# Resident slices of the second expert weights, and engines of some small steps, in an attention and mixture-of-experts kernel

## The chip, the cores and the metric

The kernel runs on one core of a Trainium2 chip. Five engines share the work: TensorE (PE in the rows, with its weight loads as PEld), VectorE (DVE), ScalarE (ACT), GpSimd (POOL) and SyncE (SP), which here only issues DMAs. The metric is device time in microseconds (us), the median of several runs.

## The reference

Three stages follow each other. `x` is 8 batches × 8 heads × 512 tokens × 64, `state` is 8 × 8 × 32 × 64.

```python
scores = scale * x @ state.T;  a = softmax(scores, -1);   xread = a @ state
scores2 = scale * state @ x.T; a2 = softmax(scores2, -1); sread = a2 @ x
y = concat([xread, sread], axis=2)          # 8 batches x 544 rows x 512
h = y @ w_in                                # 512 -> 2048
g = where(h >= 1, h, where(h <= -1, 0, (h + 1) ** 2 / 4))
z = g @ w_out                               # 2048 -> 512, 4352 rows
logits = z @ phi                            # 32 slots: 8 experts x 4
d = softmax(logits, 0);  slot_input = d.T @ z
slot_out[e] = relu(slot_input[e] @ w1[e]) @ w2[e]     # w1: 512 x 1024, w2: 1024 x 512
out = softmax(logits, 1) @ slot_out
```

The softmax over all rows (`axis 0`) means that no row of the output can be made before all rows have passed `h`; the two expert layers then work on 32 slots only, and the output is a small matrix product for 4352 rows of 512.

## The kernel before

**Loop over batches.** `b` runs from 0 to 8. For `b` from 0 to 7 a step works on the 512 token rows of a batch; `b` = 8 (`b == B`, the "state block") works on the 256 state rows of all batches. Inside, `m` runs over 16 blocks of 128 hidden columns (`hstep`). For each `m`, TensorE sums `h` into one of three PSUM banks; ScalarE makes `c = relu(h / 2 + 1/2)`; `c` is squared; VectorE makes `g = min(max(h, 1), c)` (L592) and later transposes `g` (L612, `tstep`). Who squares is a letter for each `m` in the strings `gv0` (`b` = 0), `gv1`, `gv`, `gv7` (`b` = 7) and `gvS` (state block): `S` is ScalarE, `E` is GpSimd (L568), and `B` is a third form in which VectorE clamps `h` (L563), ScalarE squares and VectorE adds (L596).

**First two steps.** While `b` = 0 runs, the 64-bit words of `w_in` and `w_out` are turned into floats (`conv_win`, `conv_wo`: lines 154 to 172, and byte copies on ScalarE and GpSimd). Tables (`cpos`, `at0`, `V0`, `E0`, `T0`, `attA`, `Vn`, `x2` and others) say at which `m` a piece of this work is written down. For `b` = 0 and 1 and for everything from `b` = 8 on, a scheduler makes each engine's order from that; for `b` = 2 to 7 TensorE's order is as written.

**State block.** `wsplit(m)` splits 128 columns of `w_in` into a high part (a copy, L519 or on ScalarE) and a low part (a subtraction, L520), for three products each in `hstep` (L546). The two letters of `wS[m]` name the engines of the two parts: `A` ScalarE, `D` VectorE, `P` GpSimd. There are two buffers, so the split for `m` can begin when the products for `m` − 2 are done.

**Last stage.** Weights come in slices of 1 MB (128 × 2048 floats): 16 of `w1`, and 16 of `w2`, of which 0 to 7 make columns 0 to 255 of `slot_out` (half 0) and 8 to 15 the columns 256 to 511 (half 1). Six `w2` slices, the last six of `order`, are loaded in the large tile `gp` as soon as the transposed `g` there has been used (`ends`); the other 26 slices are streamed through places that `give` frees. All loads and nearly all stores go through SP's one queue, in program order. `slot_out(dh)` sums the eight slices of a half (tile `SO`, L1088), resident ones first, and spreads the sum to all partitions (`SR`, L1095). `combine` then makes output rows: four products of 128 rows into four banks (`oV`, `oH`, `oX`, `oE`), two copied out by VectorE (L1128) and two by ScalarE, and stores (L1132). `c0` and `c1` make half rows (256 columns, 1 KB of an output row) for pairs of batches; `cw` makes whole rows for the batches in `whole`, for which both halves must be there. The string `so` sets the order: `0` and `1` are a slice of half 0 and half 1, `c` is a pair of half rows of half 0; what is left follows in the order half 1, `c0`, `cw`, `c1`.

```python
r0 = CFG["r0"]
kept = [list(range(8 - r0, 8)), list(range(10 + r0, 16))]
order = [i for i in range(16) if i not in kept[0] + kept[1]] + kept[0] + kept[1]
```

With `r0` = 0 the resident slices are 10 to 15, all of half 1.

Of the kernel before, what the change touches and what calls it, by code (L numbers as in the profile page):

```python
# [13 lines left out]
PSUM = bass.MemoryType.PSUM  # L14


CFG = {'no': 1, 'nl': 0, 'n0': (1, 12), 'nw': 512, 'nj': 'CABD', 'cw': (2, 2, 2, 4, 5, 6, 6, 7, 8, 8, 9, 11, 12, 13, 14, 15), 'pr': (0, 4, 6), 'a0n': 5, 'w1p': (), 'r0': 0, 'sw': 1, 'whole': (4, 5, 6, 7), 'em': 8, 'lE': (0, 5, 8, 11), 'sV': (0, 4, 9, 12), 'sE': (7, 11, 15), 'sS': (1, 3, 5, 7), 'sN': 13, 'sM': (14, 14), 'gv7': 'EESESSSEESSSEEEE', 'cpos': (0, 0, 1, 2, 2, 3, 3, 7, 8, 10, 10, 10, 14, 14), 'at0': (4, 4, 7, 7, 9, 13, 14, 14, 14, 15), 'lP0': ((0, 1), (1, 0), (3, 0), (3, 1)), 'lP1': ((1, 0), (1, 1), (2, 0), (2, 1), (3, 0)), 'gv1': 'EEEEEEEEEESEEEES', 'f32': (0, 1, 2, 3), 'wsm': 14, 'xsP': 1, 'eng': ('PE',), 'wt8': (7, 8, 9, 10, 11, 12, 13, 14), 'wte': 'DA', 'wb': 12, 'gv6': (3, 5, 15), 'lP': ((0, 0), (0, 1), (1, 0), (2, 0), (3, 1)), 'attA': (3, 3, 9, 9, 9, 10, 10, 12), 'attB': (1, 11, 11, 12, 13), 'attN': (14, 15), 'dv': (3, 7, 8), 'fl': -0.484375, 'hp': 2000, 'att7': (3, 5, 6, 7, 8, 10), 'og': 1, 'n3': 1, 'n3m': 10, 'wS': ('DP', 'PP', 'AD', 'PD', 'AP', 'DP', 'AP', 'AD', 'AD', 'DP', 'AD', 'AP', 'AP', 'AD', 'PD', 'AD'), 'xsm': 12, 'k0': 0, 'rg': 6, 'spg': 0, 'att0': 6, 'att': 7, 'V0': (1, 2, 4), 'Vn': (1, 2, 10), 'Vx': 12, 'wn': 'H', 'wsev': 'adad', 'conv': (4, 8, 9, 11, 12, 13, 19, 21, 24, 26, 28, 32, 36, 40, 44, 48, 52, 56, 60), 'todo': [1, 1, 1, 2, 0, 0, 0, 3, 0, 0, 2, 2, 1, 1, 0, 0], 'E0': ((0, 7), (0, 14), (0, 15), (1, 1)), 'T0': ((0, 9), (0, 14), (1, 1), (1, 2)), 'sm0': 6, 'E': 1, 'sm': 1, 'tqB': (5, 9, 13), 'GP': 0, 'pe': (3,), 'psH': 3, 'gtpX': (0, 7), 'tq0': (13, 15), 'keep': (2, 3, 4, 5), 'x2': (1, 0), 'natm': 1, 'warm': 26, 'bounce7': (0, 3), 'split': 1, 'wt': 0, 'so': '1011110001000010c1cc1', 'smm': (0, 0, 1, 2, 8, 10, 12), 'tqv': (), 'tqvm': 0, 'first': 'x', 'apath': 2, 'f32c': 1, 'place': 1, 'attm': (3, 6, 7, 8, 9, 12), 'subPm': True, 'loDm': False, 'bounce': (0, 1, 2, 3), 'bq': ('s', 's'), 'xq': 's', 'nat': ((1, 11), (2, 2), (2, 3), (2, 11), (3, 2), (3, 4), (3, 9), (4, 2), (4, 3), (4, 9), (5, 2), (5, 3), (5, 9), (6, 2), (6, 4), (6, 9)), 'subP': (1,), 'mulD': (), 'loD': (), 'qlag': 0, 'gv0': 'SSEEEEEESEEEEEEE', 'gv': 'EEEEEEESEEEESEEE', 'gvS': 'BEBBBBBBBBBSBEBB'}


@with_exitstack  # L20
def kernel(
# [20 lines left out]
    def pool(name, bufs, **kw):  # L42
        return ctx.enter_context(tc.tile_pool(name=name, bufs=bufs, **kw))
# [6 lines left out]
    small = pool("small", 2)  # L50
    psH = pool("psH", CFG["psH"], space=PSUM)
    psE = pool("psE", 1, space=PSUM)
    psV = pool("psV", 1, space=PSUM)
    psX = pool("psX", 5 - CFG["psH"], space=PSUM)
    dram = pool("dram", 1, space=bass.MemoryType.DRAM)
# [58 lines left out]
    def group(calls, after=(), chain=False):  # L114

        first = mm(**calls[0])  # L116
        for i in after:
            tc.add_manual_dep(first.ins, i.ins.name, SYNC, reason="side by side")
        with tc.high_priority(CFG["hp"]):
            last = first  # L120
# [5 lines left out]
    def act(out, in_, func=ACTF.Copy, **kw):  # L126
        return nc.scalar.activation(out=out, in_=in_, func=func, **kw)  # L127
# [21 lines left out]
    def words(i, dst):  # L149

        w = stage[i].bitcast(U32).rearrange("p (f w) -> p f w", w=2)
        if i in CFG["dv"]:
            d = dst.bitcast(U32)
# [9 lines left out]
        r = rim.bitcast(U8).rearrange("p (f w) -> p f w", w=4)  # L163
        act(r[:, :, 0], b[:, :, 3], scale=2.0 ** -5, bias=CFG["fl"])
        if i in CFG["pr"]:
            nc.gpsimd.tensor_copy(out=r[:, :, 3], in_=b[:, :, 7])
# [1025 lines left out]
```

## Time and profile before

| | us |
|---|---|
| runs | 482.29, 480.94, 481.89 |
| median | 481.89 |
| profiled execution | 481.2 |
| its span, first to last instruction | 479.4 |

| engine | busy us | share of the span |
|---|---|---|
| PE | 435.4 | 91% |
| DVE | 374.4 | 78% |
| ACT | 289.2 | 60% |
| POOL | 239.5 | 50% |

The table is an average over stages that have different limits: DMA is full in the first 48 us and again from about 380 us on, VectorE is full from 36 to 72 us, and TensorE is full from 60 to 400 us. 93.00 MB go through SP's queue. What a change in a stage is worth has to be read in that stage. 1.8 us of the profiled execution lie outside its span.

### The profile page before, as it was taken

The page shows a single profiled execution, that of the slowest core. Times are in us where ns is not written, and L with a number is a line of the kernel's source. Part 1 is how long each engine was busy: PE and PEld are TensorE (multiplying, and loading weights), DVE is VectorE, ACT ScalarE, POOL GpSimd, SP SyncE. Part 2 cuts the span into 40 slices and gives each one's busy share as a digit, 9 for nine tenths or more (in the row PEclk, how much of TensorE's full clock was granted, in tenths as well). Part 3 has the DMA queues.
Part 4 walks back from the last instruction along what each step waited for, and adds up shares of the span by engine and source line. Part 5 has one row for each costly group of instructions (what it writes and reads, how often), then busy time and mean ns, then how long its engine had stood idle before and what let it go on. Part 6 is the DMA issues. An engine that isn't in the chain of part 4 may idle for free.

```text
span 479.4 us, 10721 instructions
## 1 busy us (share of the span) xinstructions
PE 435.4 (91%) x4336; PEld 247.3 (52%) x4336; DVE 374.4 (78%) x667; ACT 289.2 (60%) x528; POOL 239.5 (50%) x217
## 2 busy tenths in 40 slices
PE   5689899999999999999999999999999997999850
PEld 2433345456565565655556555565557685435330
DVE  2999999896999998999799899878878655430260
ACT  1876996647775875886697587565654464220350
POOL 4243447865774973885497388464146231220030
PEclk9899999999999999999999999999999999999995
DMA  8999822011403613342351346025053598999698
GB/s 304 420 420 420 338 89 89 19 71 27 151 18 132 250 44 133 114 196 61 127 210 46 133 144 252 3 90 176 2 211 124 198 404 335 349 424 414 255 355 314
DMA packets 19809, 94.21 MB, mean 197 GB/s; under 512 B 1840, under 2 KB 6320, under 8 KB 11184
## 3 DMA queue, kind: packets, MB, share of 16 engines
q1 hardware_dynamic: 19504, 93.00, 51.0%
q8 instruction: 34, 0.56, 0.5%
q0 software_dynamic: 256, 0.52, 0.5%
q14 instruction: 15, 0.12, 0.1%
HBM read 80.41 MB, written 13.11 MB: 195 GB/s over the span
## 4 chain that ended last, share of the span: by engine, by line
PE 49%; DVE 28%; DMA 6%; ACT 5%; issue 5%; POOL 4%; ACTq 0%; SPq 0%; POOLq 0%; DVEq 0%
PE h L538 17%; DVE gp L612 6%; DVE g L592 5%; PE h L546 5%; PE E L116 3%; DMA w<-in_w_dram 3%; PE FV L122 3%; PE V L116 3%; PE h L1053 3%; POOL c L568 2%; PE h L529 2%; PE FX L122 2%; DVE mx L294 2%; DMA wb<-in_won_dram 2%; DVE z L335 1%
## 5 line engine op out<-in xcount | busy, mean ns | idle before, releaser
L538 PE MATMUL h<-a,v 128*128 128x512 f32 x672 | 175.5, 405 | 2.3 <-DVE g L592 2.0
L568 POOL TENSOR_TENSOR c<-c 128x512 f32<-128x512 f32 x106 | 114.6, 1084 | 97.1 <-ACT c L127 95.3
L538 PEld LDWEIGHTS h<-a,v 128*128 128x128 f32 x672 | 120.3, 188 | 77.9 <-issue 19.5
L127 ACT ACTIVATE c<-h,half 128x512 f32<-128x512 f32 x128 | 88.3, 691 | 71.0 <-PE h L538 54.6
L592 DVE SCALAR_TENSOR_TENSOR g<-h,c 128x512 f32<-128x512 f32 x112 | 74.7, 668 | 20.1 <-POOL c L568 17.0
L612 DVE STREAM_TRANSPOSE gp<-g 128x512 f32<-128x512 f32 x112 | 78.0, 699 | 1.1
L485 POOL TENSOR_TENSOR v<-Vs,v 128x512 fp32r<-128x512 f32 x30 | 41.7, 1389 | 9.5 <-ACT Vs L127 9.5
L127 ACT ACTIVATE v<-V 128x512 fp32r<-128x512 f32 (+1 forms) x64 | 38.1, 602 | 8.1 <-PE V L122 4.1
L116 PE MATMUL V<-win,st_t 64*32 64x512 f32 x64 | 34.0, 611 | 4.1 <-ACT att L127 3.7
L122 PE MATMUL V<-win,st_t 64*32 64x512 f32 x448 | 36.3, 612 | 0.0
L122 PE MATMUL FX<-gp,dR 32*32 32x512 f32 x512 | 35.6, 598 | 0.0
L122 PE MATMUL FV<-gp,dR 32*32 32x512 f32 x496 | 35.4, 597 | 0.0
L529 PE MATMUL h<-spare,v 128*128 128x512 f32 x64 | 32.5, 644 | 2.2 <-DVE gp L592 2.0
L122 PE MATMUL E<-g,wp 128*32 128x512 f32 x168 | 29.5, 602 | 0.0
L116 PE MATMUL E<-g,wp 128*32 128x512 f32 x56 | 29.1, 602 | 0.0
L337 POOL TENSOR_TENSOR att<-att,z 128x512 f32<-128x512 f32 x16 | 17.2, 1076 | 18.1 <-DVE z L336 18.1
L546 PE MATMUL h<-XSh,v 128*128 128x256 f32 x128 | 25.2, 289 | 0.1
L127 ACT ACTIVATE spare<-wb 128x512 uint8<-128x512 uint8 x32 | 24.0, 785 | 1.0 <-DMA wb<-in_won_dram 1.0
L1128 DVE COPY o<-oV 128x512 f32<-128x512 f32 x5 | 3.5, 691 | 26.5 <-PE oH L122 26.3
L529 PEld LDWEIGHTS h<-spare,v 128*128 128x128 f32 x64 | 11.9, 202 | 20.2 <-issue 13.5
L546 PEld LDWEIGHTS h<-XSh,v 128*128 128x128 f32 x128 | 20.2, 189 | 2.6 <-DVE g L592 0.8
L375 POOL TENSOR_TENSOR a<-att,a 128x512 fp32r<-128x512 f32 x14 | 19.6, 1418 | 1.1 <-ACT a L127 1.1
(245 smaller groups left out, 813.9 us busy)
## 6 DMA issues: line engine op xcount, KB each, us to landing
w<-in_w_dram SPq DMA_DIRECT2D x22, 1024.0 KB, 9.6
xn<-in_xn_dram SPq DMA_DIRECT2D x8, 1024.0 KB, 4.8
wb<-in_won_dram SPq DMA_DIRECT2D x8, 1024.0 KB, 5.0
xs<-in_xs_dram SPq DMA_DIRECT2D x7, 1024.0 KB, 4.8
gp<-in_w_dram SPq DMA_DIRECT2D x6, 1024.0 KB, 7.4
gp<-in_wout_dram SPq DMA_DIRECT2D x5, 1024.0 KB, 11.7
wb<-in_win_dram SPq DMA_DIRECT2D x4, 1024.0 KB, 12.8
wo<-wb SPq DMA_DIRECT2D x8, 512.0 KB, 3.7
```

The lines of the kernel that those rows point to most:

```text
L116: first = mm(**calls[0])
L122: e = mm(**c)
L127: return nc.scalar.activation(out=out, in_=in_, func=func, **kw)
L337: (nc.vector if b in CFG["mulD"] else nc.gpsimd).tensor_tensor(out=t3, in0=t3, in1=z1.unsqueeze(2).to_broadcast([128, 16, 32]), op=ALU.mult)
L375: (nc.vector if b in CFG["loD"] or b > 1 and CFG["loDm"] else nc.gpsimd).tensor_tensor(out=lo[:, G, :], in0=raw[G], in1=hi[:, G, :], op=AL ...
L485: nc.gpsimd.tensor_tensor(out=lo[:, G, :], in0=Vs, in1=hi[:, G, :], op=ALU.subtract)
L529: mm(out=h, lhsT=Vt[0, c][0][:, G, 128 * mm_:128 * mm_ + 128], rhs=araw[0][G], start=(G == 0), stop=(G == 1))
L538: mm(out=h, lhsT=v[:, G, f], rhs=a[:, G, :], start=(k == 0), stop=(k == 5))
L546: mm(out=h, lhsT=w[:, j, :], rhs=x[:, j, :], start=(k == 0), stop=(k == 11))
L568: nc.gpsimd.tensor_tensor(out=c, in0=c, in1=c, op=ALU.mult)
L592: gI[b, m] = nc.vector.scalar_tensor_tensor(out=g, in0=h, scalar=1.0, in1=c, op0=ALU.max, op1=ALU.min)
L612: nc.vector.transpose(out=gd_of(b, m), in_=gT[b, m])
```

## The change

Only the table of settings is changed (one line of code; here its changed keys stand below each other).

```diff
 CFG = {
...
-'r0': 0, 'whole': (4, 5, 6, 7), 'so': '1011110001000010c1cc1',
+'r0': 3, 'whole': (6, 7),       'so': '111000000000ccc111111',
-'gv7': 'EESESSSEESSSEEEE', 'gvS': 'BEBBBBBBBBBSBEBB',
+'gv7': 'EESEESSEEESSEEEE', 'gvS': 'BEBBBEEESSSBEBBB',
-'gv0': 'SSEEEEEESEEEEEEE',
+'gv0': 'ESSESEEESEEEEEEE',
-'wS': ('DP', 'PP', 'AD', 'PD', 'AP', 'DP', 'AP', 'AD', 'AD', 'DP', 'AD', 'AP', 'AP', 'AD', 'PD', 'AD'),
+'wS': ('AP', 'PP', 'AD', 'AP', 'DP', 'DP', 'PP', 'DD', 'AP', 'DP', 'AD', 'AP', 'DD', 'AD', 'DD', 'DP'),
-'pr': (0, 4, 6), 'a0n': 5, 'x2': (1, 0), 'V0': (1, 2, 4), 'Vn': (1, 2, 10),
+'pr': (0, 3, 4, 6), 'a0n': 4, 'x2': (1, 3), 'V0': (1, 3, 4), 'Vn': (0, 3, 9),
-'cpos': (0, 0, 1, 2, 2, 3, 3, 7, 8, 10, 10, 10, 14, 14), 'at0': (4, 4, 7, 7, 9, 13, 14, 14, 14, 15),
+'cpos': (0, 0, 1, 1, 2, 2, 3, 7, 8, 9, 10, 10, 13, 14), 'at0': (4, 4, 7, 7, 9, 13, 14, 15, 15, 15),
-'E0': ((0, 7), (0, 14), (0, 15), (1, 1)), 'T0': ((0, 9), (0, 14), (1, 1), (1, 2)),
+'E0': ((0, 8), (0, 14), (0, 14), (0, 15)), 'T0': ((0, 12), (0, 14), (0, 15), (1, 0)),
-'lP0': ((0, 1), (1, 0), (3, 0), (3, 1)), 'attA': (3, 3, 9, 9, 9, 10, 10, 12),
+'lP0': ((1, 1), (2, 1), (3, 1)), 'attA': (3, 4, 7, 9, 9, 9, 11, 12),
...
 }
```

The resident slices become 5, 6, 7 and 13, 14, 15, three of each half; streamed are 0 to 4, then 8 to 12. Batches 0 to 5 are stored in half rows, 6 and 7 in whole rows.

On TensorE at the end of the program (`w` is a streamed slice, the rows begin with the last part of half 0) the order before is:

```order
L1088 MATMUL SO<-w_7_4632,hTD 32x256 x8
L1088 MATMUL SO<-w_8_4638,hTD 32x256 x4
L1095 MATMUL SR<-tail,cst_t 128x256
L1088 MATMUL SO<-w_8_4639,hTD 32x256 x4
L116 MATMUL oV<-tail,LT 128x256
```

and with the change:

```order
L1088 MATMUL SO<-w_4_4612,hTD 32x256 x2
L1088 MATMUL SO<-w_8_4620,hTD 32x256 x8
L1095 MATMUL SR<-tail,cst_t 128x256
L1088 MATMUL SO<-w_9_4626,hTD 32x256 x8
L116 MATMUL oV<-tail,LT 128x256
```

Half 0 closes (`SR`) behind slice 8 in both, but slice 8 is now the sixth of the ten streamed ones instead of the ninth, and three slices (10, 11, 12) come behind the first products for output rows.

SP's queue at the end (`out_dram` rows of 256 are half rows) is before:

```order
L814 DMA w_8_4639<-in_w_dram 128x1024
L814 DMA w_9_4646<-in_w_dram 128x2048
L1132 DMA out_dram<-o 512x1x256 x4
L1132 DMA out_dram<-o 128x2048 x4
L1132 DMA out_dram<-o 512x1x256 x4
```

and with the change:

```order
L814 DMA w_11_4639<-in_w_dram 128x1024
L814 DMA w_12_4646<-in_w_dram 128x2048
L1132 DMA out_dram<-o 512x1x256 x6
L1132 DMA out_dram<-o 128x2048 x2
L1132 DMA out_dram<-o 512x1x256 x6
```

All stores stay behind all loads in the queue; six half stores instead of four come first.

On VectorE at the end of `b` = 7 (L592 makes `g`, L612 transposes it, L487 makes the low part of the next `v`, L519 is the copy of `wsplit(0)`), one piece of the difference:

```order
-L592 SCALAR_TENSOR_TENSOR g<-h,c 128x512 x2
-L612 STREAM_TRANSPOSE gp<-g 128x512 x2
-L487 TENSOR_TENSOR v_715<-V,v_715 128x512
-L519 CAST v_568<-win_103 128x512
-L487 TENSOR_TENSOR v_715<-V,v_715 128x512
+L592 SCALAR_TENSOR_TENSOR g<-h,c 128x512
+L612 STREAM_TRANSPOSE gp<-g 128x512
+L592 SCALAR_TENSOR_TENSOR g<-h,c 128x512
+L487 TENSOR_TENSOR v_705<-V,v_705 128x512
+L612 STREAM_TRANSPOSE gp<-g 128x512
+L487 TENSOR_TENSOR v_705<-V,v_705 128x512
```

The copy L519 leaves VectorE's queue ahead of the second L487.

On GpSimd in `b` = 0 (L166 is a byte copy of a weight conversion, L568 a square), one piece of the difference:

```order
 L166 COPY LT<-gp 128x1024
+L568 TENSOR_TENSOR c<-c 128x512
 L166 COPY LT<-wb_110 128x1024
-L568 TENSOR_TENSOR c<-c 128x512 x6
+L568 TENSOR_TENSOR c<-c 128x512 x4
```

The square of `m` = 0 comes in between two byte copies, and the squares of `m` = 2 and `m` = 4 go to ScalarE.

## Rows read from the trace of the kernel before

**Rows 1.** The page, 40 equal slices of the span: DMA engines' busy tenths.

```profile
DMA  8999822011403613342351346025053598999698
```

**Rows 2.** Windows: stretch, length, PE, PEld, DVE, ACT, POOL busy, clock, DMA share, GB/s.

```profile
364.00:398.00 34.00, 33.23 (x377) 26.44 (x374) 23.19 (x54) 18.11 (x36) 10.72 (x10) 1.00 0.75 284
398.00:402.00 4.00, 3.56 (x31) 3.31 (x29) 3.06 (x6) 1.71 (x4) 0.76 (x1) 1.00 0.49 159
...
408.00:411.00 3.00, 2.74 (x44) 1.40 (x40) 0.92 (x2) 0.77 (x2) 0.52 (x1) 1.00 0.60 199
411.00:448.00 37.00, 33.61 (x438) 15.72 (x430) 8.96 (x14) 4.87 (x11) 5.14 (x3) 1.00 1.01 414
448.00:453.00 5.00, 5.00 (x58) 2.89 (x50) 2.48 (x4) 2.60 (x6) 0.00 (x0) 1.00 0.16 62
...
469.00:471.00 2.00, 0.00 (x0) 0.00 (x0) 0.00 (x0) 0.00 (x0) 0.00 (x0) 0.50 1.02 430
471.00:477.00 6.00, 0.00 (x0) 0.00 (x0) 0.00 (x0) 0.00 (x0) 0.00 (x0) 0.50 1.02 348
```

**Rows 3.** Timeline of the end: start, length, engine, line, [idle before <-releaser].

```profile
442.77 1.07 PE L1088 MATMUL SO<-w,hTD 128*32 128x256 f32 x16 [0.75 <-DMA w<-in_w_dram]
...
448.38 0.48 PE L116 MATMUL oV<-tail,LT 32*128 32x256 f32 x1
...
450.32 0.59 PEld L1088 LDWEIGHTS SO<-w,hTD 128*32 128x32 f32 x16 [0.33 <-DMA w<-in_w_dram]
...
451.40 20.45 SPq L1132 DMA_DIRECT2D out_dram<-o  x12
...
453.55 0.69 PE L116 MATMUL oV<-tail,LT 32*128 32x512 f32 x1 [0.47 <-ACT tail L127]
```

**Rows 4.** The chain that ended last: start, length, what (b = 7 and state block).

```profile
352.74 0.64 ACT c L127
...
358.81 4.41 PE h L538 x18
364.22 3.03 PE h L546 x24
...
393.69 0.64 ACT v L127
```

**Rows 5.** Timeline of the end of b = 7 and of the state block.

```profile
355.81 1.75 DVE L519 CAST v<-win 128x512 fp32r<-128x512 f32 x1
...
372.74 0.66 PE L660 MATMUL dRp<-cst_t,eS 128*128 128x128 f32 x4 [0.67 <-ACT eS L127]
...
372.86 1.29 POOL L520 TENSOR_TENSOR v<-win,v 128x512 fp32r<-128x512 f32 x1 [1.09 <-DVE v L519]
```

**Rows 6.** Waits of SP's queue from 383 to 413 us: in total, times, longest.

```profile
SPq L814 <- DVE v L520: 7.6, 1, 7.6
```

**Rows 7.** Timeline of b = 0.

```profile
33.74 3.66 PE L529 MATMUL h<-spare,v 128*128 128x512 f32 x4 [2.04 <-DVE gp L592]
...
43.11 3.70 PE L529 MATMUL h<-spare,v 128*128 128x512 f32 x8
...
36.78 1.21 DVE L156 SCALAR_TENSOR_TENSOR win<-wb,win 128x1024 uint32<-128x1024 uint32 x1
...
41.58 1.95 DVE L156 SCALAR_TENSOR_TENSOR wD<-ast,wD 128x1024 uint32<-128x1024 uint32 x1
...
30.26 2.27 POOL L166 COPY LT<-wb 128x1024 uint8<-128x1024 uint8 x1 [4.68 <-DVE win L172]
...
41.24 1.20 POOL L568 TENSOR_TENSOR c<-c 128x512 f32<-128x512 f32 x1 [2.00 <-ACT c L127]
```

**Rows 8.** Windows, columns as in Rows 2.

```profile
34.00:37.00 3.00, 3.00 (x4) 1.13 (x5) 3.00 (x4) 1.85 (x5) 1.23 (x1) 0.50 1.00 418
...
340.00:364.00 24.00, 23.91 (x235) 14.10 (x233) 19.75 (x29) 13.20 (x23) 10.77 (x9) 1.00 0.30 111
```

**Rows 9.** The page's groups: line, engine, out<-in, count | busy, mean ns | idle before.

```profile
L568 POOL TENSOR_TENSOR c<-c 128x512 f32<-128x512 f32 x106 | 114.6, 1084 | 97.1 <-ACT c L127 95.3
```

More of the change, by code (lines that the diff above doesn't have):

```diff
@@ L14 @@
 PSUM = bass.MemoryType.PSUM
-CFG = {'no': 1, 'nl': 0, 'n0': (1, 12), 'nw': 512, 'nj': 'CABD', 'cw': (2, 2, 2, 4, 5, 6, 6, 7, 8, 8, 9, 11, 12, 13, 14, 15), 'pr': (0, 4, 6), 'a0n': 5, 'w1p': (), 'r0': 0, 'sw': 1, 'whole': (4, 5, 6, 7), 'em': 8, 'lE': (0, 5, 8, 11), 'sV': (0, 4, 9, 12), 'sE': (7, 11, 15), 'sS': (1, 3, 5, 7), 'sN': 13, 'sM': (14, 14), 'gv7': 'EESESSSEESSSEEEE', 'cpos': (0, 0, 1, 2, 2, 3, 3, 7, 8, 10, 10, 10, 14, 14), 'at0': (4, 4, 7, 7, 9, 13, 14, 14, 14, 15), 'lP0': ((0, 1), (1, 0), (3, 0), (3, 1)), 'lP1': ((1, 0), (1, 1), (2, 0), (2, 1), (3, 0)), 'gv1': 'EEEEEEEEEESEEEES', 'f32': (0, 1, 2, 3), 'wsm': 14, 'xsP': 1, 'eng': ('PE',), 'wt8': (7, 8, 9, 10, 11, 12, 13, 14), 'wte': 'DA', 'wb': 12, 'gv6': (3, 5, 15), 'lP': ((0, 0), (0, 1), (1, 0), (2, 0), (3, 1)), 'attA': (3, 3, 9, 9, 9, 10, 10, 12), 'attB': (1, 11, 11, 12, 13), 'attN': (14, 15), 'dv': (3, 7, 8), 'fl': -0.484375, 'hp': 2000, 'att7': (3, 5, 6, 7, 8, 10), 'og': 1, 'n3': 1, 'n3m': 10, 'wS': ('DP', 'PP', 'AD', 'PD', 'AP', 'DP', 'AP', 'AD', 'AD', 'DP', 'AD', 'AP', 'AP', 'AD', 'PD', 'AD'), 'xsm': 12, 'k0': 0, 'rg': 6, 'spg': 0, 'att0': 6, 'att': 7, 'V0': (1, 2, 4), 'Vn': (1, 2, 10), 'Vx': 12, 'wn': 'H', 'wsev': 'adad', 'conv': (4, 8, 9, 11, 12, 13, 19, 21, 24, 26, 28, 32, 36, 40, 44, 48, 52, 56, 60), 'todo': [1, 1, 1, 2, 0, 0, 0, 3, 0, 0, 2, 2, 1, 1, 0, 0], 'E0': ((0, 7), (0, 14), (0, 15), (1, 1)), 'T0': ((0, 9), (0, 14), (1, 1), (1, 2)), 'sm0': 6, 'E': 1, 'sm': 1, 'tqB': (5, 9, 13), 'GP': 0, 'pe': (3,), 'psH': 3, 'gtpX': (0, 7), 'tq0': (13, 15), 'keep': (2, 3, 4, 5), 'x2': (1, 0), 'natm': 1, 'warm': 26, 'bounce7': (0, 3), 'split': 1, 'wt': 0, 'so': '1011110001000010c1cc1', 'smm': (0, 0, 1, 2, 8, 10, 12), 'tqv': (), 'tqvm': 0, 'first': 'x', 'apath': 2, 'f32c': 1, 'place': 1, 'attm': (3, 6, 7, 8, 9, 12), 'subPm': True, 'loDm': False, 'bounce': (0, 1, 2, 3), 'bq': ('s', 's'), 'xq': 's', 'nat': ((1, 11), (2, 2), (2, 3), (2, 11), (3, 2), (3, 4), (3, 9), (4, 2), (4, 3), (4, 9), (5, 2), (5, 3), (5, 9), (6, 2), (6, 4), (6, 9)), 'subP': (1,), 'mulD': (), 'loD': (), 'qlag': 0, 'gv0': 'SSEEEEEESEEEEEEE', 'gv': 'EEEEEEESEEEESEEE', 'gvS': 'BEBBBBBBBBBSBEBB'}
@@ new lines @@
+CFG = {'no': 1, 'nl': 0, 'n0': (1, 12), 'nw': 512, 'nj': 'CABD', 'cw': (2, 2, 2, 4, 5, 6, 6, 7, 8, 8, 9, 11, 12, 13, 14, 15), 'pr': (0, 3, 4, 6), 'a0n': 4, 'w1p': (), 'r0': 3, 'sw': 1, 'whole': (6, 7), 'em': 8, 'lE': (0, 5, 8, 11), 'sV': (0, 4, 9, 12), 'sE': (7, 11, 15), 'sS': (1, 3, 5, 7), 'sN': 13, 'sM': (14, 14), 'gv7': 'EESEESSEEESSEEEE', 'cpos': (0, 0, 1, 1, 2, 2, 3, 7, 8, 9, 10, 10, 13, 14), 'at0': (4, 4, 7, 7, 9, 13, 14, 15, 15, 15), 'lP0': ((1, 1), (2, 1), (3, 1)), 'lP1': ((1, 0), (1, 1), (2, 0), (2, 1), (3, 0)), 'gv1': 'EEEEEEEEEESEEEES', 'f32': (0, 1, 2, 3), 'wsm': 14, 'xsP': 1, 'eng': ('PE',), 'wt8': (7, 8, 9, 10, 11, 12, 13, 14), 'wte': 'DA', 'wb': 12, 'gv6': (3, 5, 15), 'lP': ((0, 0), (0, 1), (1, 0), (2, 0), (3, 1)), 'attA': (3, 4, 7, 9, 9, 9, 11, 12), 'attB': (1, 11, 11, 12, 13), 'attN': (14, 15), 'dv': (3, 7, 8), 'fl': -0.484375, 'hp': 2000, 'att7': (3, 5, 6, 7, 8, 10), 'og': 1, 'n3': 1, 'n3m': 10, 'wS': ('AP', 'PP', 'AD', 'AP', 'DP', 'DP', 'PP', 'DD', 'AP', 'DP', 'AD', 'AP', 'DD', 'AD', 'DD', 'DP'), 'xsm': 12, 'k0': 0, 'rg': 6, 'spg': 0, 'att0': 6, 'att': 7, 'V0': (1, 3, 4), 'Vn': (0, 3, 9), 'Vx': 12, 'wn': 'H', 'wsev': 'adad', 'conv': (4, 8, 9, 11, 12, 13, 19, 21, 24, 26, 28, 32, 36, 40, 44, 48, 52, 56, 60), 'todo': [1, 1, 1, 2, 0, 0, 0, 3, 0, 0, 2, 2, 1, 1, 0, 0], 'E0': ((0, 8), (0, 14), (0, 14), (0, 15)), 'T0': ((0, 12), (0, 14), (0, 15), (1, 0)), 'sm0': 6, 'E': 1, 'sm': 1, 'tqB': (5, 9, 13), 'GP': 0, 'pe': (3,), 'psH': 3, 'gtpX': (0, 7), 'tq0': (13, 15), 'keep': (2, 3, 4, 5), 'x2': (1, 3), 'natm': 1, 'warm': 26, 'bounce7': (0, 3), 'split': 1, 'wt': 0, 'so': '111000000000ccc111111', 'smm': (0, 0, 1, 2, 8, 10, 12), 'tqv': (), 'tqvm': 0, 'first': 'x', 'apath': 2, 'f32c': 1, 'place': 1, 'attm': (3, 6, 7, 8, 9, 12), 'subPm': True, 'loDm': False, 'bounce': (0, 1, 2, 3), 'bq': ('s', 's'), 'xq': 's', 'nat': ((1, 11), (2, 2), (2, 3), (2, 11), (3, 2), (3, 4), (3, 9), (4, 2), (4, 3), (4, 9), (5, 2), (5, 3), (5, 9), (6, 2), (6, 4), (6, 9)), 'subP': (1,), 'mulD': (), 'loD': (), 'qlag': 0, 'gv0': 'ESSESEEESEEEEEEE', 'gv': 'EEEEEEESEEEESEEE', 'gvS': 'BEBBBEEESSSBEBBB'}
```

## The prediction

> **What bounds the kernel now.** I read the page first: DMA is full in the first tenth of the span and in its last fifth, and thin between [rows 1]. Then windows by stage. From 411 to 448 us the weights stream at 414 GB/s with a DMA share of 1.01; from 448 to 453 us the share is 0.16; then the stores fill it again, to 477 us [rows 2]. So the end of the program is bound by DMA, with one hole of 5 × (1 − 0.16) = 4.2 us between the last weights and the first stores. The timeline tells why: the first products for output rows start at 448.38 and the first store is issued at 451.40, while the last weight slice is used at 450.32 [rows 3]. Two smaller holes stand before, 398 to 402 us (share 0.49, that is 2.0 us idle) and 408 to 411 us (0.60, 1.2 us) [rows 2]; in the first, SP's queue stood 7.6 us for VectorE's low part of `w_in` [rows 6]. What TensorE and VectorE save in the state block (364 to 404 us) can therefore still reach the end, up to those 3.2 us. From 60 to 364 us TensorE is the bound (23.91 of 24 us busy in the last 24 [rows 8]), and before that the conversions.
>
> **The end of the program.** Bytes are the same: 26 streamed slices, six resident ones, the same stores. What moves is the moment at which stores are ready. A slice of 1.049 MB takes 1.049 / 414e-3 = 2.5 us [rows 2]. Half 0 now needs the first five of the ten streamed `w2` slices, so it is complete 5 × 2.5 us before the last one, at 437.8 us instead of 446 us. The order puts the first output products behind the seventh slice, 3 × 2.5 us before 450.3, which is the one used at 442.77 [rows 3]. With 0.6 us for its products and 3.0 us from products to first store (451.40 − 448.38 [rows 3]) the first store is issued at 446.4 us, before the weights run out at 448. `c0` is now six half stores, 3.1 MB, which at 348 GB/s [rows 2] is 9.0 us of DMA work, to 457 us. The whole rows behind it start their products 3.2 us after the last slice (453.55 − 450.32) and issue 3.0 us later, at 456.6 us [rows 3]: the hole is closed, but with less than a microsecond to spare. That is −4.2 us.
>
> Against it stands the price of half rows for two more batches. The stretch 471 to 477 us writes half rows at 348 GB/s, 469 to 471 us whole rows at 430 GB/s [rows 2]. 2.10 MB cost 6.03 us by the one and 4.88 us by the other: +1.15 us. The sum here is −3.0 us. Its bounds: −4.2 us if the rate does not depend on the row, −1.5 us if the whole rows come 1.5 us after `c0` has drained.
>
> The Trainium skill ("DMA: Bandwidth & Descriptors", Specifications) puts the smallest transfer at line rate at 512 B, so 1 KB pieces of a row should cost nothing extra. By that rule this term would be −4.2 us and the forecast 1.15 us lower; the two rates just read speak against it, and the sum goes by them.
>
> **The state block.** Three waits of TensorE. (1) At the end of `b` = 7, VectorE copies for `wsplit(0)` from 355.81 to 357.56 us [rows 5], ahead of the low part that TensorE needs at 358.81 [rows 4]. In the change ScalarE makes this copy and the low part comes over a microsecond earlier. After the six products that precede (0.246 us each, 18 in 4.41 us [rows 4]) TensorE would have gone on 0.4 us sooner: −0.4 us. (2) `dRp` waits 0.67 us for `eS` [rows 5]; the change lets ten more products pass first, so this wait goes. What is late next is GpSimd's low part for `m` = 5, done at 374.15 us [rows 5], which then is needed at about 373.8: −0.3 us net. (3) The split of `m` = 12 on ScalarE and GpSimd holds TensorE near 393.7 us [rows 4]; with `DD` it is ready before: −0.3 us. The products of the logits of `m` 0 to 3 move ahead of the large block that frees `gp`; the resident loads wait for that block, at most 0.6 us longer, and the hole at 398 us absorbs it. Sum −1.0 us; bounds −1.4 us (all three whole) and +0.6 us (`gp` comes late and nothing else helps).
>
> **The squares of b = 7.** Two go from ScalarE (0.64 us [rows 4]) to GpSimd (1.08 us [rows 9]), 0.44 us later each. TensorE has other work queued, 23.91 of 24 us [rows 8]: 0; without that cover +0.9 us.
>
> **The first two steps.** Most new numbers change nothing that is built: conversion 3 is on VectorE anyway, `lP0` is not read when `b` = 0 keeps floats, the fifth step of attention 0 is empty, and the scheduler gives almost the old order for the rest (two neighbours swap on TensorE, two pairs on VectorE; SP's queue is the same). What is left is `gv0`. The square of `m` = 0 goes to GpSimd ahead of the byte copy at 30.26 us, while VectorE is about its conversions. The two engines hold each other up there: L156 takes 1.21 us alone and 1.95 us beside the square that starts at 41.24 us [rows 7]. So the first `g`, for which TensorE stood 2.04 us until 33.74 us [rows 7], comes up to 1.1 us (one square [rows 9]) later. Half of it is returned if TensorE's clock rises when it did: from 34 to 37 us it is granted 0.50, 1.2 GHz [rows 8], and 4 products take 3.66 us where 8 take 3.70 us later [rows 7], so a microsecond not worked there is worth half of one. The square of `m` = 4 leaves GpSimd and gives VectorE 1.95 − 1.21 = 0.7 us, but is one more operation (0.64 us) before ScalarE's conversions. I take +0.5 us, near the middle of the bounds −0.6 us (only the second square counts) and +1.75 us (1.1 us and ScalarE's 0.64 us).
>
> **Sum.** −3.0 − 1.0 + 0 + 0.5 = −3.5 us. Against the profiled execution 481.2 − 3.5 = 477.7 us; against the median 481.9 − 3.5 = 478.4 us. The forecast is 478.4 us.
>
> **Rivals.**
> More gain: half rows cost nothing beside other transfers, and the state block gives all of its 1.4 us with no loss at the start: −4.2 − 1.4 = −5.6 us, 476.3 us. For it: within a stretch the rate varies by more than the difference that I charge. Against: both rates come from full shares [rows 2].
> The start eats it: +1.75 us there, and in the state block new waits take the place of the old: −3.0 + 1.75 = −1.25 us, 480.6 us. For it: VectorE is full from 36 to 72 us, as the section on the profile says, so a delay has little slack to vanish in.
> The change doesn't do what it says: TensorE's queue is in order, and pairs two and three of `c0` stand behind slices 10 and 11. If the stores of `c0` come only when the last slice has landed, the hole stays and half rows cost: +1.15 − 1.0 + 0.5 = +0.65 us, 482.5 us. Against: slice 9 is used at 442.8 us.
> Slower: GpSimd makes ten low parts in the state block instead of eight. The copy, 0.64 us [rows 4], and the low part, 1.29 us [rows 5], with some 0.2 us between them take 2.1 us, the products of a step half of 3.03 us [rows 4]; a split can only start when the step before last is through. Where nothing else stands between on TensorE, each costs 0.6 us. Seven of the ten are exposed if none is covered: +4.2 us, and −3.0 + 4.2 + 0.5 = +1.7 us, 483.6 us. It decides from five such steps on. Against: logits, transposes and the block for `acc` stand between most of them.
>
> **How the numbers follow.** Forecast 0.60; more gain 0.14; the start 0.13; the hole stays 0.06; slower 0.07. A measurement of this kernel can tell about 0.3%, 1.45 us, from no change. Faster by more, below 480.4 us: the first two and a third of the start, 0.78. Within: the rest of the start and the hole, 0.15. Slower: 0.07. The range from 476.0 to 481.2 us takes in the larger gain and the start's case and leaves out the last two.
>
> **What would show it.** In the windows of the changed kernel no stretch of 2 us between the last weights and the end has a DMA share under 0.8, and the first store is issued some 4 us before the last slice is used. Half rows run at about 350 GB/s, whole rows at 430. `dRp` waits no more, VectorE has no L519 near 356 us, and the products of `b` = 8 end about 1 us earlier. The wait of the first `g` at 33.7 us ends 0 to 1.1 us later. I am wrong if the DMA share falls anew between `c0` and the whole rows, or if TensorE stands for GpSimd's L520.

## The result and the profile after

| | before | after |
|---|---|---|
| median, us | 482.09 (480.94 to 483.36) | 476.94 (475.79 to 479.15) |
| ratio | | 0.9902, 95% interval 0.9873 to 0.9932 |
| first profiled execution | 481.2 | 479.15 |
| second profiled execution (among the experiments) | | 475.85 |

The change takes 5.15 us off (1.0%; by the interval 3.3 to 6.1 us); forecast were 3.5 us, 478.4 us with a range from 476.0 to 481.2. The first profiled execution happened to be the longest of its six runs, the second the shortest of its six. At `b` = 7 the first is still 0.4 us ahead of the second (its first `g` starts at 330.37 us there, at 330.75 us in the second); what it loses it loses behind that, nearly all of it at the end of the program. Both are shown, since what differs there is the thing that the prediction spoke of. Line 2 of the page (DMA engines' busy tenths in 40 slices), first and second execution, to hold against [rows 1]:

```profile
DMA  8999822111403713351361336025053599999798
```

```profile
DMA  8999822010403613260361326207043499999998
```

Windows of both (stretch, length, PE, PEld, DVE, ACT, POOL busy, clock, DMA share, GB/s); they answer to the row of 448 to 453 us in [rows 2]. First execution, then second:

```profile
443.00:448.00 5.00, 5.00 (x52) 3.22 (x53) 1.64 (x3) 0.95 (x2) 0.00 (x0) 0.66 0.70 287
448.00:453.00 5.00, 5.00 (x64) 2.60 (x59) 2.23 (x4) 2.41 (x5) 0.00 (x0) 1.00 0.74 252
```

```profile
364.00:396.00 32.00, 31.94 (x369) 25.66 (x368) 22.84 (x52) 15.70 (x32) 13.98 (x15) 1.00 0.75 286
...
443.00:448.00 5.00, 5.00 (x60) 2.89 (x53) 3.77 (x6) 2.77 (x5) 0.00 (x0) 1.00 1.00 396
448.00:453.00 5.00, 4.02 (x40) 1.57 (x38) 0.28 (x1) 1.36 (x3) 0.00 (x0) 1.00 1.05 360
464.00:470.00 6.00, 0.00 (x0) 0.00 (x0) 0.00 (x0) 0.00 (x0) 0.00 (x0) 0.50 1.05 358
```

In the second execution there is no hole left: the DMA share is 1.00 and 1.05, where from 448 to 453 us it was 0.16 [rows 2]. In the first one 5 × 0.30 + 5 × 0.26 = 2.8 us are still idle. The timeline says why (start, length, engine, line, [idle before <-releaser]); first execution, then second, each from slice 9 to the first products of whole rows:

```profile
442.98 1.28 PE L1088 MATMUL SO<-w,hTD 128*32 128x256 f32 x16 [2.30 <-DMA w<-in_w_dram]
444.19 0.79 PE L116 MATMUL oV<-tail,LT 32*128 32x256 f32 x1
...
454.84 0.69 PE L116 MATMUL oV<-tail,LT 32*128 32x512 f32 x1 [0.47 <-ACT tail L127]
...
448.16 23.40 SPq L1132 DMA_DIRECT2D out_dram<-o  x14
```

```profile
441.04 1.07 PE L1088 MATMUL SO<-w,hTD 128*32 128x256 f32 x16 [0.47 <-DMA w<-in_w_dram]
442.04 0.48 PE L116 MATMUL oV<-tail,LT 32*128 32x256 f32 x1
...
451.55 0.69 PE L116 MATMUL oV<-tail,LT 32*128 32x512 f32 x1 [0.47 <-ACT tail L127]
...
445.06 22.84 SPq L1132 DMA_DIRECT2D out_dram<-o  x14
```

The last row of each is SyncE's queue: its start is the issue of the first store, at 451.40 us before [rows 3]. In the first execution slice 9 came 2 us late (TensorE stood 2.30 us for it), and just then TensorE was granted 1.2 GHz (clock 0.66 over 443 to 448 us, at 0.50 from 444 to 446), so that the work between the first products and the first store was drawn out, from 445.06 − 442.04 = 3.02 us to 448.16 − 444.19 = 3.97 us. Neither returned in the second execution. Of the eleven other traces of this document one alone, that of the state block alone, has a stretch at 1.2 GHz between 440 and 453 us.

For the parts to be told apart, five moments were read from the one trace that each run left: the start of the first `g` of `b` = 7 (L592), of the products `LRs` behind the state block (L672), the landing of the last weight slice, the issue of the first store and the landing of the last. "State" is `LRs` less `b` = 7, "weights" the last slice less `b` = 7, "tail" the last store less the last slice.

| kernel | state | weights | first store less last slice | tail |
|---|---|---|---|---|
| before | 73.05 | 118.98 | +1.18 | 27.98 |
| after, first | 71.39 | 120.05 | −2.26 | 25.84 |
| after, second | 71.38 | 118.00 | −3.70 | 24.24 |
| end only | 73.03 | 119.19 | −3.44 | 25.43 |
| state block only | 71.36 | 117.73 | +2.52 | 29.23 |
| start only | 73.05 | 118.83 | +1.17 | 27.96 |
| end and state, old start | 71.37 | 117.70 | −3.43 | 24.66 |
| state, last two splits only | 73.03 | 120.52 | +1.17 | 28.40 |
| state, the rest only | 71.38 | 117.78 | +1.20 | 27.93 |
| half rows for 0 to 3 | 71.36 | 117.51 | −2.09 | 25.94 |
| two resident slices a half | 71.40 | 117.56 | −1.69 | 25.94 |
| `SR` first | 71.36 | 119.07 | −3.40 | 24.26 |
| squares of `b` = 0 only | 73.03 | 119.32 | +1.18 | 28.09 |

"State" is the same to 0.04 us wherever its settings are the same, so it is worth more than the medians of some six runs, which scatter by 1 to 2 us.

### The profile page after: what moved, and what is told of

The parts are those of the page before. It is cut to its first block, busy times and chain, and to the rows that moved or that the text cites. A ratio compares the mean times of both kernels' runs of the same rounds, so it can differ in the third digit from the quotient of the medians.

```text
span 477.3 us, 10760 instructions
## 1 busy us (share of the span) xinstructions
PE 438.5 (92%) x4352; PEld 250.3 (52%) x4352; DVE 372.9 (78%) x664; ACT 288.4 (60%) x526; POOL 245.4 (51%) x222
## 4 chain that ended last, share of the span: by engine, by line
PE 51%; DVE 29%; DMA 7%; issue 4%; POOL 3%; ACT 2%; ACTq 0%; SPq 0%; POOLq 0%; DVEq 0%
PE h L538 19%; DMA w<-in_w_dram 6%; DVE gp L612 6%; DVE g L592 5%; PE h L546 5%; PE E L116 4%; PE FV L122 4%; PE V L116 3%; PE FX L122 2%; PE h L529 2%; POOL c L568 2%; DVE mx L294 2%; PE FV L116 1%; DVE win L172 1%; DVE z L335 1%
## 5 line engine op out<-in xcount | busy, mean ns | idle before, releaser
L568 POOL TENSOR_TENSOR c<-c 128x512 f32<-128x512 f32 x107 | 116.8, 1095 | 99.6 <-ACT c L127 97.8
L592 DVE SCALAR_TENSOR_TENSOR g<-h,c 128x512 f32<-128x512 f32 x112 | 74.7, 668 | 19.6 <-POOL c L568 16.9
L612 DVE STREAM_TRANSPOSE gp<-g 128x512 f32<-128x512 f32 x112 | 78.2, 700 | 1.2
L116 PE MATMUL V<-win,st_t 64*32 64x512 f32 x64 | 33.4, 601 | 4.0 <-ACT att L127 3.6
L529 PE MATMUL h<-spare,v 128*128 128x512 f32 x64 | 34.1, 671 | 1.9 <-DVE gp L592 0.9
L122 PE MATMUL V<-win,st_t 64*32 64x512 f32 x448 | 35.7, 601 | 0.0
L1136 POOL DMA_DIRECT2D out_dram<-o x8 | 4.1, 518 | 35.4 <-DVE o L1128 35.4
```

Of the source, the lines that this page charges most:

```text
L122: e = mm(**c)
L529: mm(out=h, lhsT=Vt[0, c][0][:, G, 128 * mm_:128 * mm_ + 128], rhs=araw[0][G], start=(G == 0), stop=(G == 1))
L568: nc.gpsimd.tensor_tensor(out=c, in0=c, in1=c, op=ALU.mult)
L592: gI[b, m] = nc.vector.scalar_tensor_tensor(out=g, in0=h, scalar=1.0, in1=c, op0=ALU.max, op1=ALU.min)
L612: nc.vector.transpose(out=gd_of(b, m), in_=gT[b, m])
```

## The experiments

**The end alone.** The kernel before with

```diff
-'r0': 0, 'whole': (4, 5, 6, 7), 'so': '1011110001000010c1cc1',
+'r0': 3, 'whole': (6, 7),       'so': '111000000000ccc111111',
```

> The kernel before with the three settings of the last stage alone (three resident slices of each half, batches 0 to 5 in half rows, the new order of slices and products). Theory (the prediction's term): -3.0 us against the kernel before (hole before the stores closed, -4.2; half rows of two more batches, +1.15). Rival 1, half rows cost nothing: -4.2. Rival 2, the hole stays as the two profiles seem to show (DMA share 0.70 and 0.74 in 443 to 453 us after the change): between -0.5 and +0.5. The measured gain of the whole change is 5.15 us.

477.91 us, before 481.99 (ratio 0.9904, 0.9884 to 0.9923): −4.1 us. The windows of this run show the hole gone:

```profile
443.00:448.00 5.00, 5.00 (x76) 3.16 (x72) 3.13 (x6) 2.17 (x4) 0.00 (x0) 1.00 1.01 409
448.00:453.00 5.00, 4.04 (x38) 2.04 (x36) 0.64 (x2) 1.96 (x4) 0.00 (x0) 1.00 1.05 362
```

So the mechanism is the forecast one, and the half-open hole of the first profile of after is not the rule (rival 2 falls). By its median (of four runs) the gain is that of free half rows (rival 1); by its trace, where the tail falls by 27.98 − 25.43 = 2.55 us, it is not. The two leave −2.6 to −4.1. The trace of this run understates the gain: the DMA engines are nearly idle over the last 2 us before its last store lands, at 475.03 us,

```profile
473.00:474.00 1.00, 0.00 (x0) 0.00 (x0) 0.00 (x0) 0.00 (x0) 0.00 (x0) 0.50 0.20 69
474.00:475.00 1.00, 0.00 (x0) 0.00 (x0) 0.00 (x0) 0.00 (x0) 0.00 (x0) 0.50 0.05 16
```

while in the second execution of after they are so only in the last one (share 0.88 from 471 to 472 us, 0.09 from 472 to 473, last landing 472.99). That is some 0.7 us of the 1.2 us by which the two tails differ.

**The state block alone.** The kernel before with the new `gv7`, `gvS` and `wS`.

> The kernel before with the settings of the state block alone (who squares in its 16 steps and at the end of b = 7, who splits w_in). Theory: -1.0 us, three PE waits gone. From the trace after, the gs of the state block are 1.0 us earlier against those of b = 7, so -1.0 is also what a plain sum of places gives. Rival: nothing (within 0.4 us), because the weights of the last stage still arrive when SyncE's queue lets them, not when the state block ends.

479.07 us (0.9936, 0.9917 to 0.9955): −2.9 us, more than the theory and its rival allowed. The block is 73.05 − 71.36 = 1.69 us shorter and the weights end 1.25 us earlier. The rival falls: the weights do follow. Its profile is a disturbed one: the hole is still there in this kernel, and a stretch at 1.2 GHz falls into it, where TensorE is what the stores wait for:

```profile
446.00:448.00 2.00, 2.00 (x14) 0.54 (x14) 0.00 (x0) 0.38 (x1) 0.00 (x0) 0.50 0.25 102
448.00:450.00 2.00, 2.00 (x36) 1.54 (x36) 0.84 (x2) 0.12 (x1) 0.00 (x0) 0.99 0.00 0
450.00:452.00 2.00, 2.00 (x18) 1.01 (x20) 1.64 (x3) 1.46 (x3) 0.00 (x0) 1.00 0.00 0
```

14 products fill the stretch that 18 to 36 fill at 2.4 GHz behind it. That profiled execution was the longest of the six, 480.68 us.

**The start alone.** The kernel before with the new `gv0` and the new tables of the first two steps (`pr`, `a0n`, `x2`, `V0`, `Vn`, `cpos`, `at0`, `E0`, `T0`, `lP0`, `attA`).

> The kernel before with the settings of the first two steps alone (who squares in b = 0 and all tables of the conversion). The prediction's term: +0.5 us (first square on GpSimd). The trace after says otherwise: from b = 0, m = 8, on every g is 0.55 us earlier, so a gain of about 0.55 us is now expected, and up to 0.85 if what b = 4 shows belongs to it. Rival: the 0.55 us are scatter of one profile, then within 0.3 us of the kernel before.

481.15 us in twelve runs; ratio 1.0001, 0.9976 to 1.0026. The rival holds: no difference that can be measured. The runs alone, uncertain by 1.2 us, would not exclude the forecast +0.5 either; what speaks against it are the traces. The 0.55 us that the first profile of after seemed to win are scatter of the kernel before: at `m` = 8 of `b` = 0, `g` starts at 55.40 to 55.59 us in the six profiles with all new start settings, at 55.12 to 55.93 us in the six with the old ones, and the profile of before is the latest of all (55.93). The means, 55.51 and 55.43 us, differ by 0.1 us.

**Fewer half rows.** The changed kernel with `'whole': (4, 5, 6, 7)`.

> The changed kernel with batches 4 to 7 in whole rows as before the change (four half stores ahead instead of six). Theory, half rows dearer by 0.58 us a batch: two batches fewer give 1.15 us back, but four half stores of 1.54 us, begun at 449.4 us, end at 455.6 and whole rows are first issued at 457.85, so 2.2 us of DMA are empty: +1.1 us against the changed kernel. Rival, half rows cost no more than whole ones: +2.2. Rival, the time is bound by something else at the end (the first whole rows on PE): 0.

478.51 us (0.992, 0.9902 to 0.9938), 1.6 us more than the changed kernel's 476.94 and 2.2 more than its 476.27 in the next comparison; forecast +1.1. By the ratios to the kernel before, 0.9920 and 0.9902, it is 0.9 us more, and the intervals overlap, so the times do not choose between the theory and the rival of +2.2. The windows show the second hole where it was expected, and some of the first:

```profile
446.00:448.00 2.00, 2.00 (x22) 1.13 (x23) 0.97 (x2) 1.38 (x3) 0.00 (x0) 1.00 0.46 177
452.00:454.00 2.00, 1.44 (x14) 0.37 (x12) 1.53 (x3) 0.80 (x2) 0.00 (x0) 1.00 0.87 295
454.00:456.00 2.00, 1.94 (x16) 0.66 (x16) 1.34 (x3) 1.02 (x3) 1.33 (x3) 1.00 0.51 199
```

Idle are 1.08 + 0.26 + 0.98 = 2.3 us, and the tail is only 25.94 − 24.24 = 1.7 us longer than in the second execution of after. So by the traces whole rows for two batches give 0.6 us back. Half rows cost about half of the 1.15 us that the prediction charged.

**End and state block, old start.** The kernel before with the settings of the first two experiments together.

> The kernel before with the settings of the last stage and of the state block, without those of the first two steps. The two alone gave -4.1 and -2.9 us. If they add up and the start is worth nothing: -7.0 us against the kernel before, 475.0. Theory: they share one hole. With the state block faster the weights land earlier, but the products that the first stores wait for do not come earlier by as much, so the DMA engines run dry again for 1 to 2 us; then about -5.2, as the whole change, and the start settings are worth 0 (within 0.5).

476.43 us beside 481.25 before (0.9902, 0.9879 to 0.9925): −4.8 us, no different from the changed kernel in the same comparison (476.27). The start settings are worth nothing, and the sum of −7.0 is not reached. But the theory of the shared hole is not what the trace shows either: the first store is issued 3.43 us ahead of the last slice and no stretch runs dry. Within this trace the weights are 118.98 − 117.70 = 1.3 us earlier and the tail 27.98 − 24.66 = 3.3 us shorter, 4.6 us together, which is what its median says. What doesn't fit are the medians of the two alone, which promised 7.0. With the −1.3 to −1.5 us that most of the state block's settings give in twelve runs further down, in place of −2.9, the sum is −5.4 to −5.6 us, inside the interval of this run (−3.6 to −5.8 us).

**`SR` first.** The changed kernel; the first product of the first streamed slice of half 1 is ordered behind `SR` of half 0.

```diff
-                mm(out=SO[c:c + 32, :], lhsT=hTD[:, ft, 32 * e:32 * e + 32],
+                p = mm(out=SO[c:c + 32, :], lhsT=hTD[:, ft, 32 * e:32 * e + 32],
...
+                if dh and e == es[r0] and "SR" in run:
+                    tc.add_manual_dep(p.ins, run["SR"].ins.name, ORDER, reason="side by side")
...
-        mm(out=SR, lhsT=R, rhs=SOs, start=True, stop=True)
+        run["SR"] = mm(out=SR, lhsT=R, rhs=SOs, start=True, stop=True)
```

> The changed kernel with one product more to the front on TensorE: the spread of half 0 (SR, L1095) goes ahead of slice 8 instead of behind it, so the first products for output rows stand 2.5 us (one slice) less far behind the close of half 0. Theory: what is left of the hole (DMA share 0.70 to 0.79 in 443 to 448 us, 1.0 to 1.5 us of DMA) closes, -1.0 to -1.5 us against the changed kernel. Rival: the whole rows then come too late instead (their first issue is at 454.3 to 457.9 us, and six half stores of 1.5 us begun 1.3 us earlier end at 457): 0. Rival: the order of the two on TensorE decides nothing, since slice 8 is there before the sum is copied: 0, and the first store is issued no earlier.

476.92 us (0.9909, 0.9892 to 0.9925): no gain. The last rival holds, for a reason not given in it: slice 9, and not `SR`, stands ahead of the first products in either order, and the first store is issued 3.40 us ahead of the last slice, as in the kernel without the change of order (3.70). There was no hole to close.

**Two resident slices of each half.** The changed kernel with `'r0': 2, 'so': '1111000000000ccc11111'`.

> The changed kernel with two resident slices of each half instead of three (6, 7 and 14, 15): half 0 closes one streamed slice later, the number of half rows stays. Theory (the place of the close sets the hole): first store 2.5 us later, +2 to +2.5 us against the changed kernel. Rival (half rows and not the hole make the time): 0.

477.26 us (0.9923, 0.9905 to 0.9941): +1.0 us against the changed kernel, less than the 2 to 2.5 forecast. The two intervals overlap, so what decides here is the trace. The first store comes 3.70 − 1.69 = 2.0 us later against the last slice, of which 1.16 + 0.24 = 1.4 us are idle:

```profile
446.00:448.00 2.00, 2.00 (x32) 1.14 (x31) 1.62 (x3) 1.44 (x3) 0.00 (x0) 1.00 0.42 176
448.00:450.00 2.00, 2.00 (x20) 1.05 (x16) 1.29 (x2) 1.19 (x2) 0.00 (x0) 1.00 0.88 292
```

So the place where half 0 closes sets the hole; with three slices it has some 0.6 us to spare, which the forecast left out. The rival falls, since the hole is there again with the same half rows.

**The changed kernel again.**

> The changed kernel once more, for a second profile beside its own parts in one comparison: 476.9 us within 0.5. In the first profile a slice landed 4.0 us behind the one ahead, at 442.94, and TensorE's granted clock was 0.66 in 443 to 448 us. If that belongs to the kernel it is there again; if it is scatter, slices land every 2.5 us up to 448.5, the clock is 1.00 there, and the first store is issued at about 446.3 instead of 448.16.

476.27 us (0.9902, 0.9886 to 0.9919). Slices land every 2.5 us, the clock is 1.00 through 448 us, the first store is issued at 445.06 us: the late slice and the clock of the first profile were scatter.

**The state block in two parts.** First the last two splits alone, in the kernel before; the trace of before had shown SyncE's queue standing 7.6 us for the low part of `m` = 15 [rows 6], and I thought that its release was the larger gain.

```diff
-'wS': (..., 'AP', 'AD', 'PD', 'AD'),
+'wS': (..., 'AP', 'AD', 'DD', 'DP'),
```

> The kernel before with the engines of the last two splits of w_in alone (m = 14 and 15: GpSimd's copy and ScalarE's copy go to VectorE, the last low part goes to GpSimd). The settings of the state block gave -2.9 us where three waits of TensorE were priced at -1.0. Theory of the release: the first load of the next stage stood 7.6 us for the low part of m = 15, since it lands where w_in was; these letters end that low part some 2 us earlier, so the load is issued at about 397.5 us instead of 399.61 and the weights end about 1.5 us earlier: -1.5 us (between -1.0 and -2.0). Theory of TensorE's waits (the prediction's): none of the three waits lies in these two steps: 0, within 0.3.

481.35 us (1.0000, 0.9984 to 1.0016): nothing, and the theory of the release falls. The load is issued at 399.16 us, where before it was 399.61, but all of `b` = 7 is already 0.65 us earlier in this run, so that against it the load is 0.2 us later. The low part (GpSimd, L520) cannot begin sooner, since it stands behind a square that stands for ScalarE:

```profile
397.26 0.61 POOL L568 TENSOR_TENSOR s_gc<-s_gc 128x256 f32<-128x256 f32 x1 [3.62 <-ACT s_gc L127]
397.83 1.29 POOL L520 TENSOR_TENSOR v<-win,v 128x512 fp32r<-128x512 f32 x1
```

Then all the rest of the state block's settings, with these two splits as before:

> The kernel before with the rest of the state block's settings (squares of b = 7 and 8, splits of m = 0 to 13; the last two splits as before). Theory of TensorE's waits: all of the gain is here, -1.0 by the three waits, -2.9 if everything measured comes from them. Theory of the release: TensorE's steps are 1.0 us earlier against b = 7, but the load still waits for the last low part, which moves with them by no more than that: -1.0 at most, -0.5 likely.

480.22 us in twelve runs (0.9969, 0.9955 to 0.9984): −1.3 us, −1.5 by the ratio. The block has the full gain, 71.38 against 73.05 us, and TensorE is as full as in the changed kernel:

```profile
364.00:396.00 32.00, 31.94 (x370) 25.66 (x369) 21.74 (x49) 16.79 (x34) 13.62 (x15) 1.00 0.76 291
```

So it was TensorE's idle time, as forecast, and the last two splits alone are worth nothing. Why all settings together measured −2.9 us where this part has the same block and the same landing of the weights (117.73 and 117.78) stays open; the intervals of the two ratios just touch (0.9955).

**The squares of `b` = 0 alone.** The kernel before with the new `gv0`.

> The kernel before with the squares of b = 0 alone (m = 0 and 7 to GpSimd, m = 2 and 4 to ScalarE). The prediction's term: +0.5 us. From three profiles with all start settings the first g is 0.6 to 0.75 us later and that of m = 4 is 1.1 us earlier against kernels with the old start, and by m = 8 both are equal, since VectorE is full there and has the same work. If the squares are all that acts: the same picture, and 0 within 0.5 us of the kernel before. Rival: the tables make m = 4 earlier; then here the first g alone is later and the time +0.5.

482.56 us in twelve runs (1.0019, 0.9997 to 1.0041): slower by 1 us or not at all, undecided. The picture is neither: the first `g` is not late. VectorE here, then in the second execution of after:

```profile
30.06 1.22 DVE L172 SCALAR_TENSOR_TENSOR win<-win,win 128x1024 uint32<-128x1024 uint32 x1
...
32.65 1.28 DVE L592 SCALAR_TENSOR_TENSOR gp<-h,c 128x512 f32<-128x512 f32 x2
...
30.62 1.56 POOL L568 TENSOR_TENSOR c<-c 128x512 f32<-128x512 f32 x1 [5.10 <-ACT c L127]
```

```profile
30.00 2.06 DVE L172 SCALAR_TENSOR_TENSOR win<-win,win 128x1024 uint32<-128x1024 uint32 x1
...
33.75 1.27 DVE L592 SCALAR_TENSOR_TENSOR gp<-h,c 128x512 f32<-128x512 f32 x2
...
29.65 1.32 POOL L568 TENSOR_TENSOR c<-c 128x512 f32<-128x512 f32 x1 [4.20 <-ACT c L127]
30.93 2.35 POOL L166 COPY LT<-wb 128x1024 uint8<-128x1024 uint8 x1
```

Where GpSimd's square and byte copy run through the whole of L172, it takes 2.06 us; where the square began only at 30.62 us, 1.22 us. In all six profiles with the new start settings it is 2.06 or 2.07 us and the first `g` 0.6 to 0.8 us later than the 33.01 us of before.

## Why the prediction was right, and where its sizes were off

**The end: −3.0 forecast; about −3.5 found.** The argument held step by step. With these settings of the end the first store goes out 3.4 to 3.7 us ahead of the landing of the last slice (2.26 us in the first execution of after), its issue at 445.06 us in the second execution (446.4 forecast for weights that end 1.5 us later); the hole closes, and the whole rows begin their products 2.8 us after the landing of the last slice (451.55 − 448.75), with the DMA share at 1.05 until then. In tails it is 27.98 to 24.24, 24.66 and 24.26 us in the three traces with all end and state settings that have no stretch at 1.2 GHz at the end, −3.3 to −3.7; with the end settings alone −2.55 in the trace and −4.1 in the median. The term that was mis-sized is the price of half rows: the hole of 4.2 us less 3.3 to 3.7 leaves 0.5 to 0.9 us for two batches, the experiment with fewer of them 0.6, and 1.15 was charged. The rate of half rows was read right (348 GB/s then [rows 2], 358 GB/s now from 464 to 470 us), but the price was taken as the difference to 430 GB/s from a window of only 2 us with whole rows, and that difference was too large. The same trace of before has a longer stretch with whole rows, and stores of state rows among them:

```profile
464.00:470.00 6.00, 0.00 (x0) 0.00 (x0) 0.00 (x0) 0.68 (x2) 0.00 (x0) 0.77 1.00 381
```

At 381 GB/s 2.10 MB take 5.5 us, and the price by the same sum would have been 0.5 us.

The Trainium skill's rule ("DMA: Bandwidth & Descriptors", Specifications: line rate from 512 B on) would have given −4.2 us here. The rows do not bear it out, 358 GB/s against 414 while weights stream [rows 2] and 381 with whole rows; as a price it was too low by 0.5 to 0.9 us, and mine was too high by 0.25 to 0.65.

**The state block: −1.0 forecast; −1.67 found in the block, −1.4 at the weights.** The chain of waits of the second execution, marks of TensorE from the first products of `b` = 8 to `LRs`:

```profile
363.40 3.03 PE h L546 x24
...
374.96 0.54 PE FV L116
...
385.14 1.07 PE P L756 x8
...
389.36 2.83 PE h L546 x24
...
395.35 0.33 PE E L116
...
402.30 0.52 PE LRs L672 x2
```

and of before, where the first mark stands at 364.22 us [rows 4]:

```profile
376.00 0.54 PE FV L116
...
386.45 0.99 PE P L756 x8
...
390.89 2.73 PE h L546 x23
...
397.25 0.33 PE E L116
...
404.45 0.45 PE LRs L672 x2
```

`b` = 7 begins 0.49 us earlier in this execution (330.75 for 331.24), which has to be taken off. The marks are then earlier by 0.33, 0.55, 0.82, 1.04, 1.41 and 1.66 us. The three waits named in the prediction lie in the first, second and fifth step: 0.33, 0.22 and 0.37, together 0.92 us where 1.0 was forecast. The other 0.74 us are steps in which I had named no wait. The window says the same in one number: TensorE works 31.94 of 32 us where the row from 364 to 398 us in [rows 2] has 33.23 of 34. I followed three waits, bounded the sum by those three whole (−1.4 us), and did not ask how much of the stretch was idle in all. The rows had most of it: 34 − 33.23 and, from 398 to 402 us, 4 − 3.56 [rows 2] are 1.21 us of idle TensorE. From the first mark to the last, before and then in the second execution of after, the windows are

```profile
364.22:404.45 40.23, 38.01 (x418) 30.71 (x418) 26.46 (x60) 20.48 (x40) 11.47 (x11) 1.00 0.75 281
```

```profile
363.40:402.30 38.90, 37.75 (x418) 30.70 (x418) 25.96 (x58) 18.85 (x38) 15.35 (x15) 1.00 0.78 293
```

TensorE's idle time falls from 2.22 to 1.15 us, which is 1.07 of the 1.33 us that the stretch is shorter. The rival of ten low parts on GpSimd, the slower case, did not happen: TensorE does not stand for L520.

Of the 1.67 us, 1.4 reach the landing of the last slice (mean 119.08 us behind `b` = 7 with the old settings, 117.71 with the new, without the three runs whose slices came late: the first of after, the last two splits, and `SR` first). Without leaving those three out it is 1.2 us by the means. Here the prediction was right that the holes in the DMA at 398 to 411 us let it through: the share from 398 to 402 us was 0.49 [rows 2] and is 0.93 in the second execution.

**The start: +0.5 forecast; 0 found.** The mechanism was there: GpSimd beside VectorE makes L172 2.06 us long instead of 1.22, and the first `g` comes 0.6 to 0.8 us later, inside the 0 to 1.1 us of the text. What failed is the step from there to the end. At `m` = 4 the `g` is already 1 us earlier than with the old settings (41.91 to 42.11 us in six profiles against 42.95 to 43.45 in six), at `m` = 8 they are level. So the bounds held the result, and the value taken inside them, near the middle, was wrong. The kernel with the end and state settings and the old start says the same, with 476.43 us beside the 476.27 of the whole change. Why they are level at `m` = 8 was not tried; that VectorE, full up to 60 us, has the same work either way is only an argument. The rival in which the start eats the gain falls.

**Squares of `b` = 7: 0 forecast, 0 found.** TensorE works 24.00 of 24 us from 340 to 364 us in both profiles of after.

**What would show it.** Of the signs named, the absent hole, the first store ahead of the weights, `dRp` without a wait and no copy of L519 near 356 us are all there in the second execution; in the first, the windows from 443 to 453 us showed what the text had excluded, and only a second profile told that it was that execution and not the kernel. The sum of the terms as found, −3.5 − 1.4 + 0 = −4.9 us, stands beside −5.15 and −4.98 measured in two comparisons. All three sizes erred to the same side, so the forecast missed by 1.65 us, and the measured 476.94 us lies closer to the rival of more gain (476.3) than to the forecast (478.4). That rival had the state block's 1.4 us and a start that costs nothing right; half rows without a price it had wrong.

## What to carry to other kernels

Before pricing single waits in a stage that one engine limits, take that engine's idle time in the stage from the windows: it bounds roughly what reordering can give, and what the named waits don't account for belongs in the bound. Where the end is set by DMA, look for the hole between the last load and the first store, and place the work that feeds the first stores as early as the loads allow, then stop: once the hole is shut, moving it further gives nothing. And measure a part by the distance between two marks in the trace, not by the median alone, when it is smaller than the scatter of the runs.

## What the runs showed of the hardware

TensorE's granted clock falls to 1.2 GHz for stretches of some 3 to 4 us, and not always at the same places: 34 to 37 us in the profile of before [rows 8], inside 24 to 30 us in both of after (0.73 and 0.69 over those 6 us), and from 444 us on in the first of after only. Where such a stretch is on the path, as between slice 9 and the first store, the first store came 3.1 us later (448.16 for 445.06); a late slice is included, and the part between the first products and the first store grew by 0.95 us.
